# P times V in tiles of 64 rows by 32 columns, and four PSUM banks in place of five for the shared tiles

## The chip, the cores and the metric

The kernel runs on one core of one Trainium2 chip. The metric is the device time of one execution in microseconds, the median of 3 runs. The engines are named as the profile names them: PE (the matrix engine; PEld is its weight load), DVE (vector), ACT (scalar), POOL, SP, and the DMA queues. A matmul multiplies a stationary operand (loaded first) by a moving one that streams through, and adds into PSUM, which has eight banks of 128 partitions by 512 float32.

## The reference

Two branches read the same layer-normed input of 2048 rows by 576 columns, and the output joins them:

```
xn  = layernorm(x)                                   # [2048, 576]
q,k,v = split(xn @ wqkv)                             # 32 heads of 18 columns
p   = softmax(q @ k^T * 18**-0.5)                    # 2048 x 2048 per head
s   = (p @ v, heads side by side) @ wo
g   = silu( (relu(xn @ W_gate) * (xn @ W_up)) @ W_down )   # hidden width 4608
out = x + s * g
```

All is float32. The product that the change touches is `p @ v`, one for every head.

## The kernel before, in words

**Stages.** First the projections q, k and v are made and spilled to DRAM. Then comes one long main stage in which two things are interleaved by hand: the gated layer (lines 300 to 410) and the attention (lines 440 to 620). Last come the output projection and the join.

**Units.** The gated layer is cut into 144 units: a group of 512 rows by 128 of the 4608 hidden columns. One unit (`up`, then `up_end`) is 27 pairs of matmuls over 64 rows each into two banks of their own (`pg0`, `pg1`, the pool `psG`); then ACT takes the relu (`r`, L376), DVE the product (`h`, L378), and ACT and POOL split it (`hh`). After every second unit `down` multiplies two units' `hh` by W_down (`py`, eight tiles of six matmuls), which DVE adds to `y` (L407).

**Attention.** It goes by pairs of heads (16 pairs, `u`), by 512 queries (`qc`, four) and by 128 keys (`kt`, sixteen). One head of a pair lies in the partitions 0 to 63, the other in 64 to 127. `max_steps` makes scores into a tile `pm`, and DVE takes their maxima (`mx`, L531). `exp_steps` makes the scores again with the maximum taken off into a tile `psx`, and ACT writes the exponentials as a tile `p` (L582), keys on partitions, both heads side by side. `attend` takes two key tiles at once: four matmuls, one for each key tile and head, whose stationary operand is 32 columns of `va` (18 columns of v and a column of ones, which gives the softmax's sum) and whose moving operand is `p`. Each of the four adds into its own quarter of the partitions of one bank, `po`; so eight calls of `attend` add up all keys of 512 queries.

**finish.** When the last keys are in, ACT copies `po` to `ot` (L538). Later, as a task, PE transposes `ot` (a tile `tp2`), DVE adds the two key tiles' sums (`os`, L545), takes reciprocals and scales (`rc`, `ob`).

**What sets the order.** PE's order is written out by `emit_unit`: for each of the two halves of 64 rows it spreads the unit's 27 matmuls, the `pm` and the `psx` evenly, and issues one step of the lower rows and one of the upper rows in turn. After them come all `attend` calls that are ready, in one block (two to four calls), and in every second unit `down` and the waiting tasks. Nine units make up one pair of heads; so in 135 units there is one block each, and in the last stage 32 more, of one call each. DVE, ACT and POOL take their instructions in the order in which the scheduler places them, strictly one after the other.

**Banks.** The tiles `pm`, `psx`, `py`, `tp`, `tp2` and the projections' own (`pq`, `pv`) share one pool, `psS`, whose banks are handed out in turn; a matmul that begins a tile waits until the reader of the bank's last tile is done.

```
    psS = ctx.enter_context(tc.tile_pool(name="psS", bufs=5, space=PSUM))
    psO = ctx.enter_context(tc.tile_pool(name="psO", bufs=1, space=PSUM))
    psG = ctx.enter_context(tc.tile_pool(name="psG", bufs=2, space=PSUM))
```

Of the kernel before, what the change touches and what calls it, by code (L numbers as in the profile page):

```python
# [9 lines left out]
F32 = mybir.dt.float32  # L10
F32R = mybir.dt.float32r
AF = mybir.ActivationFunctionType
ALU = mybir.AluOpType
AX = mybir.AxisListType
PSUM = bass.MemoryType.PSUM
# [4 lines left out]
def kernel(  # L20
# [10 lines left out]
    nc = tc.nc  # L31
    P = 128
    R = P // 2
    _, S, D = x.shape
# [5 lines left out]
    NT = S // P  # L40
# [6 lines left out]
    VA = 20  # L47
# [15 lines left out]
    def mm(*args, **kw):  # L63
        return tc.keep_in_program_order(nc.tensor.matmul(*args, **kw))  # L64

    def tp(*args):
        return tc.keep_in_program_order(nc.tensor.transpose(*args))  # L67

    consts = ctx.enter_context(tc.tile_pool(name="consts", bufs=1))
    dram = ctx.enter_context(tc.tile_pool(name="dram", bufs=1, space=DRAM))  # L70
    psS = ctx.enter_context(tc.tile_pool(name="psS", bufs=5, space=PSUM))
    psO = ctx.enter_context(tc.tile_pool(name="psO", bufs=1, space=PSUM))
    psG = ctx.enter_context(tc.tile_pool(name="psG", bufs=2, space=PSUM))
    ident = consts.tile([P, P], F32, name="ident")
    make_identity(nc, ident)
# [10 lines left out]
    def shared(name):  # L86
        return psS.tile([P, 512], F32, tag="one", name=name)
# [365 lines left out]
    for i in range(2):  # L453
        va = at.tile([P, NT, VA + 32], F32, name=f"va{i}")
# [80 lines left out]

    def finish(po, dst, then, *args):
        ot = two.tile([P, 512], F32, name="ot")
        nc.scalar.activation(ot, po, AF.Copy)  # L538

        def rest_():  # L540
            ps = shared("tp2")
            for j in range(4):
                tp(ps[:, j * P : (j + 1) * P], ot[:, j * P : (j + 1) * P], ident)
            os = two.tile([P, 8, VA], F32, name="os")
            nc.vector.tensor_reduce(  # L545
                os[:, :, : DH + 1],
                ps.rearrange("p (a i d) -> p a d i", i=2, d=32)[:, :, : DH + 1, :],
                axis=AX.X, op=ALU.add,
            )
            rc = two.tile([P, 8], F32, name="rc")  # L550
            nc.vector.reciprocal(rc, os[:, :, DH])
            for d in dst:
                nc.vector.tensor_tensor(
                    d.rearrange("p t (h d) -> p t h d", d=DH),
                    os[:, :, :DH].rearrange("p (t h) d -> p t h d", h=2),
                    rc.rearrange("p (t h) -> p t h", h=2).unsqueeze(3).to_broadcast([P, 4, 2, DH]),
                    ALU.mult,
                )
            then(*args)

        tasks.append((rest_, ()))
# [27 lines left out]
    po = [None]  # L589

    def attend():

        va, qc, kt, pq, done = ready.pop(0)
        if kt == 1:
            po[0] = psO.tile([P, 512], F32, name="po")
        for i in (0, 1):
            for h in (0, 1):
                s_ = 32 * (2 * h + i)
                mm(
                    po[0][s_ : s_ + 32, :], va[:, kt - 1 + i, h * VA : h * VA + 32], pq[i][:, h, :],  # L600
                    start=(kt == 1), stop=(kt == NT - 1), skip_group_check=True,
                )
        if kt == NT - 1:
            done(qc, po[0])

    def to_dram(u):
        ob = two.tile([P, NT, HW], F32, name="ob", bufs=1)

        def store(qc):
            if qc == NQ - 1:  # L610
                nc.sync.dma_start(od[:, u * HW : (u + 1) * HW].rearrange("(t p) d -> p t d", p=P), ob)

        return lambda qc, po_: finish(po_, [ob[:, qc * 4 : qc * 4 + 4, :]], store, qc)

    def emit_unit(k, ex, ns, mx, nm):
        up_weights(k + 1)
        if k % 2 and k < len(units):
            down_weights(k - 1)
            down_weights(k)
        n = KC * len(PRODUCTS) + ns + nm  # L620
        ps, gens = up(k)
        order = []
        for t in range(2):
            at_ = {}
            for cnt, gen, off in ((nm, mx, 0.0), (ns, ex, 0.25)):
                for i in range(cnt):
                    at_.setdefault(round((i + off + t * 0.5) * (n - 1) / cnt), []).append(gen[t])
            todo, ops = [], []
            for i in range(n):
                todo += at_.get(i, [])  # L630
                ops.append(todo.pop(0) if todo else gens[t])
            order.append(ops)
        for i, (l, r) in enumerate(zip(*order)):
            next(l)
            next(r)
            if i % 12 == 8:
                gate_step()
        up_end(k, ps)
        while ready:
            attend()  # L640
        if k % 2 == 0 and k:
            for _ in down(k - 1):
                pass
            run_tasks()
# [51 lines left out]
    def done15(qc, po_):  # L696
        finish(
            po_, [o5[:, qc * 4 : qc * 4 + 4, d * DT + U15 : d * DT + DT] for d in range(2)], closed.append, qc
        )
# [109 lines left out]
    for n, _ in enumerate(zip(*[exp_steps(NU - 1, h, pp, done15, True) for h in range(2)])):  # L809
        if n % 2:  # L810
            if len(ready) > 1:
                attend()
            run_tasks()
            due = min(due, 1.0) + 2.2
            while due > 0:
                c = next(outs, None)
                if c is None:
                    break
                due -= c
    while ready:  # L820
        attend()
# [31 lines left out]
```

## Time and profile before

| what | value |
|---|---|
| median of 3 runs | 2805.68 us (2805.17 to 2806.87) |
| the profiled execution | 2808.65 us, its span 2806.9 us |
| granted TensorE clock, mean | 0.992 |
| PE, DVE, ACT, POOL busy | 97%, 69%, 52%, 40% of the span |
| chain that ended last | PE 82%, DVE 9%, DMA 3%, issue 3% |
| main stage | about 370 to 2640 us |

Busy is the union of an engine's instructions. PE's instructions overlap each other, so that a busy PE may still be slowed. In a row of groups, `x` is the count, then come the busy time, the mean of one in ns, and the idle time of the engine just before them with what ended it. A row of the timeline gives the start in us, the length, the engine, the line and the tiles; `x8` means eight such in a row.

### The profile page before, as it was taken

The page shows a single profiled execution, that of the slowest core. Times are in us where ns is not written, and L with a number is a line of the kernel's source. Part 1 is how long each engine was busy: PE and PEld are TensorE (multiplying, and loading weights), DVE is VectorE, ACT ScalarE, POOL GpSimd, SP SyncE. Part 2 cuts the span into 40 slices and gives each one's busy share as a digit, 9 for nine tenths or more (in the row PEclk, how much of TensorE's full clock was granted, in tenths as well). Part 3 has the DMA queues.
Part 4 walks back from the last instruction along what each step waited for, and adds up shares of the span by engine and source line. Part 5 has one row for each costly group of instructions (what it writes and reads, how often), then busy time and mean ns, then how long its engine had stood idle before and what let it go on. Part 6 is the DMA issues. An engine that isn't in the chain of part 4 may idle for free.

```text
span 2806.9 us, 55965 instructions
## 1 busy us (share of the span) xinstructions
PE 2729.5 (97%) x22252; PEld 2081.1 (74%) x22252; DVE 1947.0 (69%) x3458; ACT 1470.5 (52%) x2730; POOL 1135.2 (40%) x845
## 2 busy tenths in 40 slices
PE   6998999999999999999999999999999999999988
PEld 4887777777777777777777777777767777777655
DVE  6325977777777777777777777777777777777542
ACT  4321155655565656565555556565645555555554
POOL 2013544444434444444444444444444444444322
PEclk9999999999999999999999999999999999999999
DMA  8745222323262322223252323232432323231344
GB/s 225 186 147 161 69 60 68 76 60 83 58 146 66 83 71 75 61 69 75 65 140 67 83 64 79 63 79 67 102 89 72 78 65 73 66 72 48 82 132 142
DMA packets 309845, 250.22 MB, mean 89 GB/s; under 512 B 76432, under 2 KB 247952, under 8 KB 309584
## 3 DMA queue, kind: packets, MB, share of 16 engines
q1 hardware_dynamic: 297800, 222.16, 32.1%
q10 hardware_dynamic: 10504, 19.76, 2.1%
q0 software_dynamic: 1280, 4.72, 0.4%
q8 instruction: 176, 2.88, 0.4%
q14 instruction: 85, 0.70, 0.1%
HBM read 201.51 MB, written 44.53 MB: 88 GB/s over the span
## 4 chain that ended last, share of the span: by engine, by line
PE 82%; DVE 9%; DMA 3%; issue 3%; ACT 1%; POOL 1%; SPq 1%; ACTq 0%; DVEq 0%; POOLq 0%
PE pg L64 25%; PE py L64 17%; PE po L64 16%; PE pm L64 10%; PE psx L64 8%; DVE mx L531 7%; PE pw L64 2%; PE tp L67 1%; PE pq L64 1%; DMA rgw<-in_A_wqkv_dram 1%; PE pv L64 1%; DVE e L428 1%; DMA x<-xTd 1%; ACT p L582 1%; PE tps L67 0%
## 5 line engine op out<-in xcount | busy, mean ns | idle before, releaser
L64 PE MATMUL pg<-x,gw 64*128 64x512 f32 x7776 | 1446.0, 397 | 14.5 <-DVE h L378 6.1
L531 DVE TENSOR_REDUCE mx<-pm 128x1 f32<-128x512 f32 x2048 | 1312.1, 684 | 175.5 <-PE pm L64 122.2
L582 ACT ACTIVATE p<-psx 128x512 f32<-128x512 f32 x2048 | 1154.0, 599 | 420.6 <-PE psx L64 314.4
L64 PEld LDWEIGHTS pg<-x,gw 64*128 64x128 f32 x7776 | 1079.3, 187 | 107.1 <-DVE h L378 7.7
L64 PE MATMUL pm<-kT,qT 54*128 54x512 f32 x2048 | 841.7, 411 | 3.3 <-DMA qT<-qd 0.9
L64 PE MATMUL psx<-qT,kT 56*128 56x512 f32 x2048 | 767.8, 401 | 4.5 <-DVE mx L531 3.2
L64 PEld LDWEIGHTS py<-dw,hh 128*128 128x128 f32 x3456 | 460.5, 188 | 61.4 <-issue 52.6
L64 PE MATMUL py<-dw,hh 128*128 128x288 f32 x3456 | 478.2, 297 | 0.0
L64 PE MATMUL po<-p,va 128*32 128x512 f32 x4096 | 474.1, 596 | 0.0
L64 PEld LDWEIGHTS pm<-kT,qT 54*128 54x128 f32 x2048 | 380.1, 186 | 124.8 <-issue 70.6
L407 DVE TENSOR_TENSOR y<-py,y 128x288 f32<-128x288 f32 x544 | 247.7, 457 | 316.5 <-PE py L64 316.5
L94 POOL CAST gw<-rg 128x1152 fp32r<-128x1152 f32 x144 | 164.7, 1144 | 652.8 <-PE pg L64 634.4
L64 PEld LDWEIGHTS psx<-qT,kT 56*128 56x128 f32 x2048 | 366.0, 186 | 50.3 <-DVE mx L531 19.0
L95 POOL TENSOR_TENSOR gw<-rg,gw 128x1152 fp32r<-128x1152 f32 x144 | 382.4, 2656 | 11.5
L94 POOL CAST dw<-rd 128x576 fp32r<-128x576 f32 x144 | 95.6, 664 | 636.4 <-PE py L64 277.3
L64 PEld LDWEIGHTS po<-p,va 128*32 128x32 f32 x4096 | 117.1, 109 | 266.5 <-issue 254.4
L500 ACT ACTIVATE nt<-tp 16x128 fp32r<-16x128 f32 x64 | 17.1, 267 | 433.3 <-PE tp L67 421.4
L95 POOL TENSOR_TENSOR dw<-rd,dw 128x576 fp32r<-128x576 f32 x144 | 205.6, 1428 | 11.5
L381 POOL TENSOR_TENSOR hh<-h,hh 128x512 fp32r<-128x512 f32 x144 | 186.5, 1295 | 15.7 <-ACT hh L380 15.7
L378 DVE TENSOR_TENSOR h<-pg,r 128x512 f32<-128x512 f32 x144 | 99.6, 691 | 98.9 <-ACT r L376 87.9
L380 ACT ACTIVATE hh<-h 128x512 fp32r<-128x512 f32 x144 | 90.8, 630 | 119.3 <-DVE h L378 119.3
L376 ACT ACTIVATE r<-pg 128x512 f32<-128x512 f32 x144 | 85.3, 592 | 80.0 <-PE pg L64 62.4
(77 smaller groups left out, 1232.7 us busy)
## 6 DMA issues: line engine op xcount, KB each, us to landing
rg<-in_B_W_gate_dram SPq DMA_DIRECT2D x144, 288.0 KB
rg<-in_B_W_up_dram SPq DMA_DIRECT2D x144, 288.0 KB
rd<-in_B_W_down_dram SPq DMA_DIRECT2D x144, 288.0 KB
x<-xTd SPq DMA_DIRECT2D x54, 256.0 KB
kT<-kd SPq DMA_DIRECT2D x372, 36.0 KB
qT<-qd SPq DMA_DIRECT2D x372, 36.0 KB
qd<-hh ACTq DMA_DIRECT2D x16, 512.0 KB
kd<-hh ACTq DMA_DIRECT2D x16, 512.0 KB
```

The costliest lines, as they stand in the source:

```text
L64: return tc.keep_in_program_order(nc.tensor.matmul(*args, **kw))
L67: return tc.keep_in_program_order(nc.tensor.transpose(*args))
L94: nc.gpsimd.tensor_copy(hi, raw)
L95: nc.gpsimd.tensor_tensor(lo, raw, hi.bitcast(F32), ALU.subtract)
L376: nc.scalar.activation(r, ps[0], AF.Relu)
L378: nc.vector.tensor_tensor(h, ps[1], r, ALU.mult)
L380: nc.scalar.activation(hh[:, 0], h, AF.Copy)
L381: nc.gpsimd.tensor_tensor(hh[:, 1], h, hh[:, 0].bitcast(F32), ALU.subtract)
L407: nc.vector.tensor_tensor(ys[j][:, cs], ps, ys[j][:, cs], ALU.add)
L428: tc.keep_in_program_order(nc.vector.reciprocal(e[:, cs], e[:, cs]))
L531: nc.vector.tensor_reduce(mx[:, h, j, c : c + 1], ps, axis=AX.X, op=ALU.max)
L582: nc.scalar.activation(pts[kt][:, h, :], ps, AF.Exp, scale=SCALE)
```

## The change

The diff, whole:

```
-    psS = ctx.enter_context(tc.tile_pool(name="psS", bufs=5, space=PSUM))
-    psO = ctx.enter_context(tc.tile_pool(name="psO", bufs=1, space=PSUM))
+    psS = ctx.enter_context(tc.tile_pool(name="psS", bufs=4, space=PSUM))
+    psO = ctx.enter_context(tc.tile_pool(name="psO", bufs=2, space=PSUM))
...
     def finish(po, dst, then, *args):
         ot = two.tile([P, 512], F32, name="ot")
-        nc.scalar.activation(ot, po, AF.Copy)
+        nc.scalar.activation(ot, po[0], AF.Copy)
+        nc.vector.tensor_tensor(ot, po[1], ot, ALU.add)
...
         if kt == 1:
-            po[0] = psO.tile([P, 512], F32, name="po")
+            po[0] = [psO.tile([P, 512], F32, name="po") for _ in range(2)]
         for i in (0, 1):
             for h in (0, 1):
                 s_ = 32 * (2 * h + i)
-                mm(
-                    po[0][s_ : s_ + 32, :], va[:, kt - 1 + i, h * VA : h * VA + 32], pq[i][:, h, :],
-                    start=(kt == 1), stop=(kt == NT - 1), skip_group_check=True,
-                )
+                for t in range(2):
+                    rr = slice(t * R, t * R + R)
+                    mm(
+                        po[0][t][s_ : s_ + 32, :], va[rr, kt - 1 + i, h * VA : h * VA + 32], pq[i][rr, h, :],
+                        start=(kt == 1), stop=(kt == NT - 1), skip_group_check=True,
+                    )
```

Each of the four matmuls of `attend`, over 128 keys, becomes two over 64 keys, one of the lower and one of the upper half of the partitions. They add into the same quarter of the partitions of two different banks. `finish` copies the one bank with ACT as before and adds the other with DVE. The bank for this comes from the shared pool, which goes from five to four.

Two places of the order show it. On PE, at the end of a unit of the second pair of queries, before (the names are those of the section above; the numbers are buffers):

```order
L64 MATMUL pg_5211<-x,gw 128x512
L64 MATMUL pg_5212<-x,gw 128x512
L64 MATMUL po<-p,va_2839 32x512 x8
L64 MATMUL pm<-kT_2829,qT 128x512
L64 MATMUL pg_5379<-x,gw 128x512
```

and in the change:

```order
L64 MATMUL pg_5270<-x,gw 128x512
L64 MATMUL pg_5271<-x,gw 128x512
L64 MATMUL po<-p,va_2839 32x512 x16
L64 MATMUL pm<-kT_2829,qT 128x512
L64 MATMUL pg_5447<-x,gw 128x512
```

The block of P times V has twice as many instructions and stands where it stood; nothing else of PE's order moves.

On DVE, where a `finish` falls at the end of a unit that has no `down`, before:

```order
L531 TENSOR_REDUCE mx<-pm 128x1 x3
L378 TENSOR_TENSOR h<-pg_5660,r 128x512
L531 TENSOR_REDUCE mx<-pm 128x1 x14
L378 TENSOR_TENSOR h<-pg_5853,r 128x512
L407 TENSOR_TENSOR y<-py,y 128x288 x8
```

and in the change:

```order
L531 TENSOR_REDUCE mx<-pm 128x1 x3
L378 TENSOR_TENSOR h<-pg_5745,r 128x512
L531 TENSOR_REDUCE mx<-pm 128x1
L539 TENSOR_TENSOR ot<-po,ot 128x512
L531 TENSOR_REDUCE mx<-pm 128x1 x13
L378 TENSOR_TENSOR h<-pg_5955,r 128x512
L407 TENSOR_TENSOR y<-py,y 128x288 x8
```

The new addition stands behind the next unit's first maximum and ahead of its other thirteen. Where a `down` follows, it stands ahead of the eight additions to `y`.

A third place is the same in both kernels; it is shown because the prediction reads the trace against it. It is PE's order inside a unit, before, with `pg0` and the `psx` and `pm` of one head on one half of the rows and `pg1` and those of the other head on the other half, in turn:

```order
L64 MATMUL psx_10566<-qT_7810,kT3_2827 128x512
L64 MATMUL pg1_10525<-x_10310,gw_10292 128x512
L64 MATMUL pg0_10524<-x_10310,gw_10292 128x512
L64 MATMUL pg1_10525<-x_10324,gw_10292 128x512
L64 MATMUL pg0_10524<-x_10310,gw_10292 128x512
L64 MATMUL pm_10573<-kT8_2837,qT_9927 128x512
L64 MATMUL pg0_10524<-x_10324,gw_10292 128x512
L64 MATMUL psx_10577<-qT_7810,kT3_2827 128x512
```

Nothing moved here: one instruction of the one half of the rows and one of the other half alternate throughout.

## The prediction

> **What bounds the kernel now.** I read the page first, then the busy time by stretches, then PE's timeline around a block of P times V, then the waits.
>
> ```profile
> span 2806.9 us, 55965 instructions
> PE 2729.5 (97%) x22252; PEld 2081.1 (74%) x22252; DVE 1947.0 (69%) x3458; ACT 1470.5 (52%) x2730; POOL 1135.2 (40%) x845
> PE 82%; DVE 9%; DMA 3%; issue 3%; ACT 1%; POOL 1%; SPq 1%; ACTq 0%; DVEq 0%; POOLq 0%
> ...
> 370.00:1300.00 930.00, 927.01 (x7563) 703.22 (x7556) 691.06 (x1205) 530.84 (x972) 406.19 (x295) 1.00 0.31 76
> 1300.00:2640.00 1340.00, 1332.74 (x10827) 1005.90 (x10827) 1000.65 (x1754) 759.89 (x1393) 581.88 (x427) 1.00 0.30 75
> ```
>
> PE is the bound: in the main stage (370 to 2640 us, the last two rows) it is busy all but 10 of 2270 us, at full clock. DVE and ACT are not, on average. But DVE ends 9% of the chain, so PE does wait for it in places. Whatever the change does is therefore read at two points: how long PE streams P times V, and how often PE waits for a bank.
>
> **P times V itself.** The groups, and PE's timeline around two blocks:
>
> ```profile
> L64 PE MATMUL po<-p,va 128*32 128x512 f32 x4096 | 474.1, 596 | 0.0
> ...
> 1515.56 0.63 PE L64 MATMUL pg<-x,gw 64*128 64x512 f32 x2
> 1516.11 0.64 PE L64 MATMUL po<-p,va 128*32 128x512 f32 x4
> ...
> 1518.28 1.47 PE L64 MATMUL po<-p,va 128*32 128x512 f32 x12
> 1519.68 0.50 PE L64 MATMUL pm<-kT,qT 54*128 54x512 f32 x1
> ...
> 1520.02 0.40 PE L64 MATMUL psx<-qT,kT 56*128 56x512 f32 x1
> ...
> 1496.11 1.92 PE L64 MATMUL po<-p,va 128*32 128x512 f32 x16
> 1497.96 0.54 PE L64 MATMUL py<-dw,hh 128*128 128x288 f32 x2
> ```
>
> The program makes 2048 such calls (16 pairs of heads, 4 groups of queries, 8 calls of `attend`, four matmuls) and the trace has 4096 records, so each is two passes. Four records last 0.64 us together where one lasts 0.60: the four column tiles start within 0.02 us and run side by side. Twelve last 1.47 us, so three such groups are (1.47 - 0.61) / 2 = 0.43 us apart. 1024 groups at 0.43 us are 440 us.
>
> The change makes 2048 calls of 128 rows into 4096 of 64 rows. Before, four tiles of 128 by 32 fill the array; after, eight of 64 by 32 fill the same array and stream the same 512 columns. If the eight run side by side, a group is eight records and still 0.43 us: **0 us**. That two halves of the rows run side by side, and don't wait for each other, is shown in other matmuls:
>
> ```profile
> 806.70 0.39 PE L64 MATMUL pg<-x,gw 64*128 64x512 f32 x1
> 806.74 0.39 PE L64 MATMUL psx<-qT,kT 56*128 56x512 f32 x1
> 806.92 0.44 PE L64 MATMUL pg<-x,gw 64*128 64x512 f32 x2
> 807.15 0.40 PE L64 MATMUL pm<-kT,qT 54*128 54x512 f32 x1
> 807.21 0.39 PE L64 MATMUL pg<-x,gw 64*128 64x512 f32 x1
> 807.39 0.39 PE L64 MATMUL psx<-qT,kT 56*128 56x512 f32 x1
> ```
>
> Matmuls of 0.39 us start two in every 0.23 us. And against the order shown above (a `psx`, four `pg`, a `pm`) one `pg` starts 0.04 us ahead of the `psx` that stands before it, and the last `pg` 0.06 us after the `pm` that stands behind it. So the two halves have queues of their own. No row shows rows and columns cut at once. I take 0; the bounds are a gain of 52 us and a loss of 72 us, both worked out next and under the rivals.
>
> **Changing tiles.** A third group begins at 1518.28 + 0.86 = 1519.14, and `pm` could start 0.43 us later, at 1519.57; it starts at 1519.68, and the next of its half 0.34 us on, where 0.23 is usual. So leaving the block costs 0.11 + 0.11 us. Entering costs 0.09: the second `pg` starts at 1515.79 (0.63 less 0.40 us after the first), `po` 0.32 us later in place of 0.23. There is one block in each of 135 units and 32 in the last stage: 167 x 0.31 = 52 us. After the change the rows (64) agree on both sides and only the columns differ. Does that save it? `po` to `py` keeps the rows (128) and changes the columns: sixteen records from 1496.11 are four groups, whose last would be through at 1496.11 + 0.46 + 3 x 0.43 = 1497.86, and `py` starts at 1497.96, 0.10 us late just as `pm` is. So the columns alone cost it, and I take 0 saved. The Trainium skill ("TensorEngine Tiling (Array Packing)", Key Properties) says that changing the tiling mode, and not merely the tile, drains the engine. By that rule too nothing is saved; if only the rows counted, the sum would be 52 us lower. The trace agrees with the rule.
>
> **The shared banks, five to four.** This term decides. The readers, and a place where PE waits today:
>
> ```profile
> L531 DVE TENSOR_REDUCE mx<-pm 128x1 f32<-128x512 f32 x2048 | 1312.1, 684 | 175.5 <-PE pm L64 122.2 <-PE pg L64 26.6
> L582 ACT ACTIVATE p<-psx 128x512 f32<-128x512 f32 x2048 | 1154.0, 599 | 420.6 <-PE psx L64 314.4 <-PE pm L64 17.2 <-PE pg L64 14.6
> ...
> 1507.86 0.74 DVE L428 RECIPROCAL e<-e 128x96 f32<-128x96 f32 x1
> 1508.52 0.63 DVE L531 TENSOR_REDUCE mx<-pm 128x1 f32<-128x512 f32 x1
> ...
> 1508.43 0.40 PE L64 MATMUL psx<-qT,kT 56*128 56x512 f32 x1
> 1508.43 0.63 PE L64 MATMUL pg<-x,gw 64*128 64x512 f32 x2
> 1509.20 0.50 PE L64 MATMUL pm<-kT,qT 54*128 54x512 f32 x1
> ...
> PEld psx L64 <- DVE mx L531: 19.0, 42, 0.9
> PEld pm L64 <- DVE mx L531: 18.7, 52, 0.6
> ```
>
> A reciprocal of the gate puts DVE behind; the maximum of an older `pm` ends at 1509.15, and only then, 0.05 us later, may `pm` at 1509.20 start in its bank. With four banks the `psx` one tile earlier, at 1508.43, needs that bank and waits 0.77 us. So the wait isn't new in kind: it comes one tile sooner.
>
> Three steps give its size. First, for each of the 4864 tiles of the pool that follow another in their bank I took the start of its first matmul less the end of the reader of the tile that four banks would put before it. With five banks the shortest distance is the 0.05 us above; with four, 1022 fall below it, by 164 us in all. Second, that counts one late reader several times, since the first wait moves the rest: in each stretch in which the reading engine never idles I keep the longest alone, and join stretches of DVE and ACT that overlap. That leaves 82 us in 300 stretches. Third, 19.0 + 18.7 = 38 us are waited today (the last two rows) and move forward with the rest. 82 - 38 = **44 us**, between 0 (all of it falls where PE waits anyway) and 164 - 38 = 126 us. I take the middle step, because readers that are late together are the rule, as in the example.
>
> **The addition in finish.** 64 times DVE adds a bank to `ot`. The nearest row is the product `h`, one bank and one SBUF operand of the same shape:
>
> ```profile
> L378 DVE TENSOR_TENSOR h<-pg,r 128x512 f32<-128x512 f32 x144 | 99.6, 691 | 98.9 <-ACT r L376 87.9 <-ACT nx L495 9.8 <-POOL dw L95 1.0
> L407 DVE TENSOR_TENSOR y<-py,y 128x288 f32<-128x288 f32 x544 | 247.7, 457 | 316.5 <-PE py L64 316.5
> 470.04 0.60 ACT L538 ACTIVATE ot<-po 128x512 f32<-128x512 f32 x1 [1.38 <-PE po L64]
> 470.36 2.08 DVE L531 TENSOR_REDUCE mx<-pm 128x1 f32<-128x512 f32 x3 [2.36 <-PE pm L64]
> 1505.07 0.49 PE L64 MATMUL pm<-kT,qT 54*128 54x512 f32 x1
> PE tp L67 <- ACT ot L538: 5.8, 5, 1.5
> ```
>
> In 29 of the 64 `down` follows, and DVE waits 317 / 544 = 0.58 us ahead of each of its eight additions: 0.69 us is hidden there. Were the cover gone, it would be 20 us. In 30 the next unit follows: ACT's copy ends at 470.64, DVE's first maximum at about 471.05, then the addition, 0.69 us, and behind it queue thirteen maxima, for whose banks PE waits. How much of 0.69 us reaches PE: a full unit's 14 `pm` and 16 `psx` take 11.04 us (1505.07 to 1516.11), so four tiles pass in 1.47 us, of which matmul, maximum and release take 0.40 + 0.68 + 0.05; 0.34 us are left. 30 x (0.69 - 0.34) = **10 us**, between 0 and 21. In the last stage PE has nothing else to do five times (last row): 5 x 0.74 = **4 us**. ACT's work is the same, and no DMA is added.
>
> **The sum.** The profiled execution took 2808.65 us, 3 us over the median of the runs. 2808.65 + 0 + 44 + 10 + 4 = 2867; less 3, **2864 us**, 2.1% slower.
>
> **Rivals.** *The row halves of a column take turns once.* If the second pass on the lower rows holds back the first on the upper rows that stands behind it, the upper rows run one pass late through the block, and each block is one pass longer: 167 x 0.43 = 72 us, 2936 us. Against it is the early start at 806.70; for it, that this was seen in full columns alone. The Trainium skill ("TensorE: Matmul & The Clock Gate", Part 3, The mechanism) says that matmuls start and end strictly in program order, which would give this or worse; the early start by 0.04 us disagrees. *Only four of eight run at once:* 440 us more, 3304 us; against it stand both halves of the argument, four columns and two rows side by side. *No change of tile any more:* 52 us less, 2812 us; against it `po` to `py`. *A pass over 64 rows streams faster*, the case on the other side: if it takes the 0.23 us of the matmuls over 64 rows, 1024 x 0.20 = 205 us go, 2659 us; it decides once a pass is under 0.43 - 58 / 1024 = 0.37 us. Against it: those matmuls are one record for each call, not two, so it is another kind of pass.
>
> **Chances.** Forecast 0.60 (2835 to 2900 by itself), turns 0.18, four at once 0.07, no change of tile 0.08, faster pass 0.05, something else 0.02. The range leaves out the faster pass, four at once and the rim of the turns: 2812 to 2945 us. A measurement of this kernel tells 0.2% (5.6 us) from no change. Faster is the faster pass and a little of the saved change of tile: 0.07; within 0.2%, the rest of that with both DVE terms near 0: 0.05; slower 0.88.
>
> **What would show it.** Right: `po` with 8192 records in groups of eight, 0.43 us apart, a block of four calls still 3.57 us to the next `pm`; PE's waits for `mx` about 80 us in place of 38, and some for `p`. Wrong: blocks of 4.0 us (turns), of 7 us (four at once) or under 3 us; `pm` following `po` without the 0.11 us; or bank waits that stay at 38 us.

## The result, and the profile after

The changed kernel takes **2881.66 us** (median of 4 runs, 2879.57 to 2883.58), the kernel before 2805.43 us beside it: a ratio of **1.0272, 95% interval 1.0254 to 1.0290**, so 76 us slower. The forecast was 2864 us, 58 us slower, in a range of 2812 to 2945 us.

The page of the changed kernel, and the main stage in its busy time by stretches:

```profile
span 2881.6 us, 63976 instructions
PE 2802.6 (97%) x26348; PEld 2079.1 (72%) x26348; DVE 1996.9 (69%) x3522; ACT 1500.7 (52%) x2730; POOL 1138.1 (39%) x845
PE 85%; DVE 10%; DMA 2%; ACT 1%; issue 1%; SPq 1%; POOL 0%; DVEq 0%; POOLq 0%; ACTq 0%
...
370.00:1300.00 930.00, 925.64 (x8878) 681.04 (x8876) 691.16 (x1199) 524.48 (x940) 396.99 (x288) 1.00 0.29 74
```

The kind of bound is the same: PE busy 97%, granted clock 1.00 in the stretch, DVE 10% of the chain where it was 9%. In the same 930 us PE gets through less beside P times V, so the stage gets longer. Where it does is read from the first and last starts of three tiles, before:

```profile
L64 PE MATMUL po<-p,va x4096: 592/592/710, 367.9 to 2785.6; 128*32 128x512 f32 x196
L64 PE MATMUL pm<-kT,qT x2048: 386/396/628, 241.7 to 2633.6; 54*128 54x512 f32 x187
L64 PE MATMUL pw<-wo,o5T x64: 288/295/610, 2701.0 to 2801.0; 128*128 128x288 f32 x64
```

and after (in such a row stand the count, the shortest, median and longest in ns, and the first and last start):

```profile
L64 PE MATMUL po<-p,va x8192: 589/589/786, 371.1 to 2858.9; 64*32 64x512 f32 x200
L64 PE MATMUL pm<-kT,qT x2048: 386/397/628, 241.0 to 2700.9; 54*128 54x512 f32 x187
L64 PE MATMUL pw<-wo,o5T x64: 288/294/609, 2769.6 to 2875.0; 128*128 128x288 f32 x64
```

From the first `po` to the last `pm`, which I call the main stage below, it is 2265.7 us before and 2329.8 after: **+64**. From the last `pm` to the last matmul it is 167.4 and 174.1: **+7**. The first `po` came 3 us later, which isn't shown to be the change's: in the experiments whose shared pool has four or five banks, it lies anywhere from 363 to 371 us.

**P times V** is a small part of this. PE's timeline in a window 0.36 us long, and then around whole blocks:

```profile
1531.25 0.66 PE L64 MATMUL po<-p,va 64*32 64x512 f32 x8
...
1531.25 1.09 PE L64 MATMUL po<-p,va 64*32 64x512 f32 x16
...
1531.25 1.95 PE L64 MATMUL po<-p,va 64*32 64x512 f32 x32
1533.13 6.63 PE L64 MATMUL py<-dw,hh 128*128 128x288 f32 x48
...
1566.71 3.66 PE L64 MATMUL po<-p,va 64*32 64x512 f32 x64
1570.31 6.64 PE L64 MATMUL py<-dw,hh 128*128 128x288 f32 x48
```

Eight records last 0.66 us together, sixteen 1.09, thirty-two 1.95: a group of eight every 0.43 us, as the groups of four before. So eight tiles of 64 by 32 run side by side. A block of two calls takes 1.88 us to the next matmul (1533.13 - 1531.25), where it was 1.85 (1497.96 - 1496.11), and a block of four calls 3.60 in place of 3.57. Over all 90 blocks of four calls the medians are 3.594 and 3.571 us: 0.023 us more, in 167 blocks 4 us.

**The waits for a bank**, in the view of the waits (us in total, times, longest):

```profile
PEld pm L64 <- DVE mx L531: 77.8, 242, 2.0
PEld psx L64 <- DVE mx L531: 26.5, 98, 0.7
PEld psx L64 <- ACT p L583: 15.0, 70, 0.5
...
PE tp L67 <- DVE ot L539: 9.1, 5, 2.1
```

Waits for `mx` go from 37.7 to 104.3 us and from 94 to 340 times. Waits of `psx` for `p` that were hardly there (0.3 us) come to 15.0, while the 7.3 us for which `pm` waited for `p` before are gone. The last row is the addition in the last stage, where PE waited 5.8 us for ACT's copy before. The groups show the same from another side:

```profile
L64 PE MATMUL pm<-kT,qT 54*128 54x512 f32 x2048 | 866.5, 427 | 9.6 <-DVE mx L531 5.2 <-DMA qT<-qd 0.7
L64 PE MATMUL psx<-qT,kT 56*128 56x512 f32 x2048 | 821.6, 420 | 2.6 <-DVE mx L531 1.4
```

before:

```profile
L64 PE MATMUL pm<-kT,qT 54*128 54x512 f32 x2048 | 841.7, 411 | 3.3 <-DMA qT<-qd 0.9 <-DVE mx L531 0.6
L64 PE MATMUL psx<-qT,kT 56*128 56x512 f32 x2048 | 767.8, 401 | 4.5 <-DVE mx L531 3.2
```

The same `pm` and `psx` last 16 and 19 ns longer on average. In the timeline of the changed kernel this is the difference between a matmul of 0.39 or 0.40 us and one of 0.50 us. PE and DVE in one stretch:

```profile
1524.54 0.40 PE L64 MATMUL pm<-kT,qT 54*128 54x512 f32 x1
...
1524.77 0.40 PE L64 MATMUL psx<-qT,kT 56*128 56x512 f32 x1
1524.83 0.50 PE L64 MATMUL pm<-kT,qT 54*128 54x512 f32 x1
...
1525.43 0.49 PE L64 MATMUL psx<-qT,kT 56*128 56x512 f32 x1
1526.03 0.50 PE L64 MATMUL pm<-kT,qT 54*128 54x512 f32 x1
...
1523.50 3.07 DVE L531 TENSOR_REDUCE mx<-pm 128x1 f32<-128x512 f32 x5
```

DVE's five maxima are (3.07 - 0.68) / 4 = 0.60 us apart and end at 1524.18, 1524.78, 1525.37, 1525.97 and 1526.57. The `pm` at 1524.83, the `psx` at 1525.43 and the `pm` at 1526.03 each start 0.05 to 0.06 us after one of these ends: PE goes at DVE's pace. Exactly these three last 0.49 to 0.50 us; the two ahead of them, which didn't wait, last 0.40.

### The profile page after: what moved, and what is told of

Same layout as the page of the kernel before. It is cut to its first block, busy times and chain, and to the rows that moved or that the text cites. A ratio compares the mean times of both kernels' runs of the same rounds, so it can differ in the third digit from the quotient of the medians.

```text
span 2881.6 us, 63976 instructions
## 1 busy us (share of the span) xinstructions
PE 2802.6 (97%) x26348; PEld 2079.1 (72%) x26348; DVE 1996.9 (69%) x3522; ACT 1500.7 (52%) x2730; POOL 1138.1 (39%) x845
## 4 chain that ended last, share of the span: by engine, by line
PE 85%; DVE 10%; DMA 2%; ACT 1%; issue 1%; SPq 1%; POOL 0%; DVEq 0%; POOLq 0%; ACTq 0%
PE pg L64 25%; PE py L64 16%; PE po L64 16%; PE pm L64 11%; PE psx L64 9%; DVE mx L531 7%; PE pq L64 2%; PE pw L64 2%; PE pv L64 2%; PE tp L67 1%; DVE e L428 1%; DMA rgw<-in_A_wqkv_dram 1%; PE tps L67 1%; ACT p L583 0%; SPq L130 0%
## 5 line engine op out<-in xcount | busy, mean ns | idle before, releaser
L64 PE MATMUL pg<-x,gw 64*128 64x512 f32 x7776 | 1493.5, 399 | 11.0 <-DVE h L378 5.3
L583 ACT ACTIVATE p<-psx 128x512 f32<-128x512 f32 x2048 | 1183.6, 598 | 462.2 <-PE psx L64 343.4
L64 PEld LDWEIGHTS pg<-x,gw 64*128 64x128 f32 x7776 | 1068.2, 187 | 85.2 <-DVE h L378 7.0
L64 PE MATMUL pm<-kT,qT 54*128 54x512 f32 x2048 | 866.5, 427 | 9.6 <-DVE mx L531 5.2
L64 PE MATMUL psx<-qT,kT 56*128 56x512 f32 x2048 | 821.6, 420 | 2.6 <-DVE mx L531 1.4
L64 PE MATMUL po<-p,va 64*32 64x512 f32 x8192 | 478.2, 593 | 0.0
L64 PEld LDWEIGHTS po<-p,va 64*32 64x32 f32 x8192 | 136.6, 106 | 250.7 <-issue 239.8
```

Of the source, the lines that this page charges most:

```text
L583: nc.scalar.activation(pts[kt][:, h, :], ps, AF.Exp, scale=SCALE)
```

## The experiments

The theory: three separate costs, banks first, then the addition, then the tiles. The rival: that the cut into tiles itself costs the time (turns, changes of tile).

**1. Banks alone.** Before, with one bank less and the eighth unused:

```
-    psS = ctx.enter_context(tc.tile_pool(name="psS", bufs=5, space=PSUM))
+    psS = ctx.enter_context(tc.tile_pool(name="psS", bufs=4, space=PSUM))
```

> The kernel before with the shared pool cut to four banks and nothing else (P times V in four tiles of 128 by 32, one bank, no addition). Theory (the fifth bank is what is lost): +50 to +62 us, about 2860 us; the matmuls that wait for a bank go from 157 to about 600, and the waits of PE's weight load for mx from 38 us to about 90. Rival A (the cut into twice as many tiles costs): at most +15 us. Rival B (the addition on DVE costs): at most +15 us.

Measured: 2861.19 us, ratio 1.0190 (1.0173 to 1.0206): **+54 us**, 53 of them in the main stage. Its waits:

```profile
PEld pm L64 <- DVE mx L531: 66.4, 212, 2.1
PEld psx L64 <- DVE mx L531: 22.3, 74, 0.7
PEld psx L64 <- ACT p L582: 18.3, 90, 0.5
```

Without any change to P times V nearly the whole picture of the changed kernel's waits is there. The missing bank is 70% of the loss (54 of 76 us).

**2. Banks and addition.** The same, and in `finish` DVE adds `po` to its own copy (numerator and denominator of the softmax both double, and the quotient stays):

```
         nc.scalar.activation(ot, po, AF.Copy)
+        nc.vector.tensor_tensor(ot, po, ot, ALU.add)
```

> As the run with four banks, and DVE also adds the bank of P times V to its copy in finish, 64 times (it adds the same bank again, so that sums and denominators both double and the quotient stays). Against the change only the cut into tiles of 64 rows is missing. Theory: 4 us under the change (its blocks are 0.02 us longer, 167 of them), that is 2874 to 2880 us, and 8 to 15 us over the run with four banks alone. Rival A: 20 us or more under the change. Rival B: 40 us or more over the run with four banks alone.

Measured: 2874.89 us, 1.0239 (1.0223 to 1.0256): 14 us over experiment 1, and 7 us under the changed kernel. By the traces the addition is 6.1 us in the main stage and 5.1 in the last; what is left to the changed kernel, 4.9 us in the main stage, is put down to the tiles, of which the longer blocks above are 4. These are differences of one profiled execution each, and the four executions of this experiment alone lie between 2871.87 and 2879.60 us, so such a share is good to some us only.

**3. The addition alone**, with five banks (only the second diff).

> The kernel before with its five shared banks and the addition on DVE in finish alone. Theory: the addition puts DVE behind by 0.69 us thirty times, and the fifth bank gives 0.37 us more of slack, so that most of it is hidden: +3 to +8 us, 2808 to 2813 us (about 4 of it from five finishes in the last stage). Rival B: +40 us or more. Rival A says nothing here.

Measured: 2813.96 us, 1.0024 (1.0015 to 1.0034): +6.4 us; in the profiled execution 2.3 in the main stage and 5.4 in the last. By the traces the addition costs the main stage a third of what it costs with four banks; the medians, 6.4 and 14 us, point the same way.

**4. The addition on POOL.** In the changed kernel ACT copies both banks, and POOL adds the copies (each of the two tiles has one buffer, where `ot` had two):

```
-        nc.vector.tensor_tensor(ot, po[1], ot, ALU.add)
+        nc.scalar.activation(ou, po[1], AF.Copy)
+        nc.gpsimd.tensor_tensor(ot, ot, ou, ALU.add)
```

> The change, but the second bank is copied by ACT into a second tile and POOL adds the two tiles (one buffer for each in place of two), so that DVE is free of the addition. Theory: 8 to 12 us under the change, 2870 to 2874 us, if ACT's second copy (0.60 us, 64 times) holds up no exponentials that PE waits for; the bank waits stay. Rival B: at or near the time of before, 2805 to 2820 us. Rival A: no difference from the change.

Measured: 2893.86 us, 1.0306 (1.0288 to 1.0325), 12 us over the changed kernel. The expectation missed. A group and its waits:

```profile
L541 POOL TENSOR_TENSOR ot<-ot,ou 128x512 f32<-128x512 f32 x64 | 82.5, 1290 | 18.1 <-ACT ou L540 18.1
...
PE tp L67 <- POOL ot L541: 20.6, 5, 9.0
...
PEld psx L64 <- ACT p L585: 30.2, 116, 0.6
```

POOL takes 1.29 us for what DVE does in 0.69, and one transpose waited 9 us for it: the last stage grew by 16 us. In that longest wait ACT's second copy ended at 2701.99 us and POOL's addition began at 2708.59; in between POOL was at work on the weights `wo` of the output projection, so there it was POOL's order and not its pace. What the single buffers add, no run separates. The main stage got shorter, by 4.4 us where the addition had cost 6.1; `psx` waits 30.2 us for `p`, 15.0 in the changed kernel, so it seems that the second copy moved some of the lateness to ACT. As far as single executions show it, most of the addition's price in the main stage does go with it, but the last stage takes back more than that.

**5. Three banks**, one execution, to see how the cost of a bank grows (`bufs=3` in the kernel before).

> The kernel before with the shared pool cut to three banks, a larger dose. Theory: the same reckoning from the trace of before that gave 82 us less 38 us for four banks gives 392 less 38 = 354 us for three, so 3160 us, with waits for p (ACT) as large as those for mx (DVE). If banks are not what PE waits for, the time would stay near that of four banks.

Measured: 3230.14 us, +424 us, where the tally of the prediction, made for three banks, gave 354.

```profile
PEld psx L64 <- DVE mx L531: 245.0, 748, 1.8
PEld pm L64 <- ACT p L582: 101.6, 417, 0.4
PEld pm L64 <- DVE mx L531: 98.2, 353, 0.7
PEld psx L64 <- ACT p L582: 89.8, 261, 1.2
```

The tally is too small here as well, and by about the same share: 354 / 424 = 0.83, and 44 / 54 = 0.81 for the first bank. Not all of it lies where the first bank's loss lay: the main stage grew by 357 us, the time ahead of the first `po` by 37 and the last stage by 27.

**6 to 8. The late reader taken away.** The prediction's example was a reciprocal of the gate that puts DVE behind. The gate, 1 / (1 + exp(-y)), can be had as 0.5 + 0.5 tanh(y / 2) from ACT and POOL, with nothing on DVE:

```
-            tc.keep_in_program_order(nc.scalar.activation(e, y, AF.Exp, scale=-1.0))
+            tc.keep_in_program_order(nc.scalar.activation(e, y, AF.Tanh, scale=0.5))
             yield
-            tc.keep_in_program_order(nc.vector.tensor_scalar(e, e, 1.0, None, op0=ALU.add))
+            nc.gpsimd.tensor_scalar(e, e, 0.5, 0.5, op0=ALU.mult, op1=ALU.add)
             for n in range(6):
                 yield
-                cs = slice(n * GP, (n + 1) * GP)
-                tc.keep_in_program_order(nc.vector.reciprocal(e[:, cs], e[:, cs]))
```

This edit in the kernel before, in the one with four banks, and in the changed kernel:

> The kernel before with five banks, where the gate's sigmoid is made as 0.5 + 0.5 tanh(y/2) by ACT and POOL, so that DVE loses 96 reciprocals of 0.735 us and 16 additions of 0.45 us. It is the same function. Theory (PE waits for a bank because something on DVE puts a maximum late): fewer late maxima, so PE's waits for mx fall from 38 us to about 20, and the time by 15 to 30 us, to 2775 to 2790 us. If the waits come from the maxima's own pace instead, less than 5 us.

> Four banks and the tiles of before, with the gate's reciprocals off DVE as above. Theory: with four banks every late maximum costs more, so the same removal is worth more than with five: 30 to 45 us under the run with four banks alone. If the maxima's own pace is what waits, less than 10 us.

> The change, with the gate's reciprocals off DVE as above. Theory: 30 to 45 us under the change, about 2842 us; if the waits come from the maxima's own pace, less than 10 us.

Measured: **2777.16 us**, 0.9895 (0.9881 to 0.9910); 2828.36 us, 1.0080 (1.0065 to 1.0095); 2851.01 us, 1.0159 (1.0142 to 1.0175). The edit is worth 29 us with five banks, 33 with four, 31 in the changed kernel. The first of the three beats both kernels. Its groups and waits:

```profile
L64 PE MATMUL psx<-qT,kT 56*128 56x512 f32 x2048 | 764.3, 398 | 0.0
...
PEld pm L64 <- ACT p L580: 8.9, 23, 0.5
PEld pm L64 <- DVE mx L529: 7.0, 22, 0.4
```

96 reciprocals and 16 additions, 68.9 + 7.2 = 76 us of DVE's work, are gone, and PE's waits for `mx` fall from 38 us to 7.2. So a late DVE is the cause of most of the waits for `mx` in the kernel before. But the gain hardly depends on the number of banks. With four banks (the second of the three) these waits stay:

```profile
PEld pm L64 <- DVE mx L529: 49.7, 192, 0.6
PEld psx L64 <- ACT p L580: 15.9, 82, 0.5
PEld psx L64 <- DVE mx L529: 6.0, 36, 0.5
```

The loss of the fifth bank therefore needs no reciprocal: without them it is 2828.36 - 2777.16 = 51 us, where it was 54. What puts the readers late then, no run separates. The five maxima shown above aren't an example of it: in the changed kernel one of the gate's instructions on DVE ends just ahead of them, at 1523.58 us, and the next starts at 1526.49.

**9 to 11. Banks of their own.** If readers of two engines hold each other's banks in one shared turn, `psx` (read by ACT) could get a pool apart, and the rest another:

```
-    psS = ctx.enter_context(tc.tile_pool(name="psS", bufs=5, space=PSUM))
+    psS = ctx.enter_context(tc.tile_pool(name="psS", bufs=3, space=PSUM))
+    psX = ctx.enter_context(tc.tile_pool(name="psX", bufs=2, space=PSUM))
```

The kernel before with 3 and 2 banks, the changed kernel with 2 and 2, and experiment 6 with 3 and 2:

> The kernel before with its five shared banks divided: psx (read by ACT) takes two in turn, pm, py and the transposes (mostly read by DVE) three; a pair of the projections takes one of each. Theory (a late maximum holds back the tiles of the other reader, because the banks go round in one turn): pm comes every 0.79 us, so three banks give 2.37 us for 0.40 + 0.68 + 0.05, a slack of 1.2 us in place of 0.7, and psx has 1.38 us for 1.05. PE's waits for mx fall from 38 us to under 10, with waits for p of up to 15 us; 2780 to 2795 us. Rival (the common turn isn't the cause, the number of banks is): 2800 us or more, since psx now has only two.

> The change with its four shared banks divided two and two in the same way. Theory: pm has 2 x 0.79 = 1.58 us for 1.13, a slack of 0.45 us in place of 0.34, and a late maximum no longer holds back psx: 10 to 25 us under the change, 2857 to 2872 us, still far over before. Rival: as slow as the change or slower, because two banks for each reader are fewer than four for both.

> Both steps on the kernel before: the gate's reciprocals off DVE, and the five banks divided three and two. Theory: without the reciprocals only about 20 us of bank waits are left, so dividing adds less than alone: 5 to 12 us under the run with the gate off DVE, 2765 to 2772 us. Rival: the division costs, 2780 us or more.

Measured: 2859.15 us, 1.0193 (1.0178 to 1.0209); 3004.15 us, 1.0714 (1.0698 to 1.0730); 2850.04 us, 1.0163 (1.0146 to 1.0180). All three lost, against the expectation, by 55, 122 and 73 us against the same kernel with one pool. The waits of the first:

```profile
PEld psx L64 <- ACT p L583: 82.7, 238, 1.1
PEld pm L64 <- DVE mx L532: 31.1, 80, 1.2
```

With two banks of its own `psx` waits 82.7 us for ACT, which the shared pool had at 0.3 us. It no longer waits for `mx` (19.0 us before), but `pm`, with three banks to itself, waits 31.1 us for it, where it was 18.7. The loss isn't mainly in the main stage: in the profiled execution the main stage is 13 us longer and the last stage 35, where no `pm` uses the other three banks and `psx` still has its two; 42.3 of its 82.7 us are there. With two and two banks the main stage itself grows, by 74 us. So in these divisions a bank that either reader may leave late was worth more than one kept for each. That the shared turn itself is the trouble isn't borne out by them; other divisions weren't run.

## Why the prediction was right or wrong

| step | forecast, us | measured, us | from |
|---|---|---|---|
| tiles of 64 by 32 | 0 | 5, of it 4 the longer blocks | trace, changed kernel less experiment 2 |
| change of tile saved | 0 | 0 | trace |
| banks, five to four | 44 | 54 (53 in the main stage) | experiment 1 |
| addition, main stage | 10 | 6 | trace, experiments 2 and 1 |
| addition, last stage | 4 | 5 | trace, experiments 2 and 1 |
| sum | 58 | 70 by these rows, 76 by the medians | |

The rows of the trace leave out the start of the main stage, which moves by some us from run to run. By medians alone the three steps are 54 for the bank, 14 for the addition (experiment 2 less 1) and 7 for the tiles (the changed kernel less experiment 2); they fall 2 us short of the 76, because the kernel before took 2807.55 us beside these experiments and 2805.43 beside the changed kernel.

**Tiles: right.** The groups of eight come 0.43 us apart, so "row halves take turns", "four at once" and "a faster pass" are all refuted. The small miss is the eight starts: they come some 7 ns apart, so that the eighth starts 0.05 us after the first, where four took 0.02. The Trainium skill ("TensorE: Matmul & The Clock Gate", Part 3, Measured speedup vs the span model) gives about 4 ns a tile; an estimate from it for the four added starts is 0.016 us a block, and 0.023 was measured.

**Changing tiles: right.** From the last start of a block to the next matmul it is 0.519 us (median), before 0.522. The step that only the columns count, taken from `po` to `py`, held, and so did the rule that the Trainium skill gives in "TensorEngine Tiling (Array Packing)", Key Properties: both sides having 64 rows saved nothing.

The Trainium skill's strict program order ("TensorE: Matmul & The Clock Gate", Part 3, The mechanism), weighed as a rival at 2936 us, isn't what the trace shows, if the two passes of a call stand together in the program: with it the upper rows' first pass couldn't start ahead of the lower rows' second, and eight records would not start within 0.05 us. The records don't name their pass, so that condition is not shown.

**Banks: right in place and mechanism, too small by 10 us.** This is the term that missed most. The place was right: waits for `mx`, some for `p`, caused by one bank less alone. The example was not typical of this loss: without the reciprocals the bank still costs 51 us (experiments 7 and 6). The Trainium skill warns of this side of such a cut ("TensorEngine Tiling (Array Packing)", Gotcha 1: PSUM Pressure: row tiles write to banks of their own); experiment 1 puts 54 us on it here. The step that failed is the tally's price of a wait, which was its lateness only. I measured, in the stretches where only `pg`, `pm` and `psx` run, each `pm` or `psx` that starts within 0.06 us of its bank's release: the time since its half's last matmul, and the time to its half's next one, each less the undisturbed 0.231 us.

| | before | four banks | after |
|---|---|---|---|
| such waits | 153 | 564 | 596 |
| median time since the last matmul, us | 0.466 | 0.260 | 0.258 |
| lateness, summed, us | 34 | 64 | 74 |
| median time to the next matmul, us | 0.337 | 0.337 | 0.337 |
| delay of the next, summed, us | 19 | 61 | 64 |

In these stretches the lateness itself grew by 30 us with four banks, less than the 44 of the tally. The delay of the following matmul, which the prediction had seen only at changes of tile ("0.34 us on, where 0.23 is usual"), grew by 42 us. Half of the 564 waits are under 0.03 us, and each still pays 0.1 us behind it. The two sums together, 72 us, exceed the 53 us by which the main stage grew; the two halves of the rows run side by side, and how much of one half's delay falls where the other waits too isn't separated by any run. By this count 44 us came near 54 partly by luck: it put the lateness too high, and left out the delay behind it. That the number of waits, and not only their length, carries the price is read from these traces; no experiment varied the one without the other.

**Addition: near.** The bounds held. Experiment 3 points to what the prediction didn't have: its price in the main stage seems to depend on the banks, 2.3 us with five and 6.1 with four, by one execution each.

**What would show it**: the 8192 records and the 0.43 us came as written; a block of four calls came at 3.60 rather than 3.57 us; waits for `mx` came to 104 us, not 80, and for `p` in `psx` to 15.

## What to carry to other kernels

Before a PSUM bank is spent on something else, take it away alone and time that: here five banks to four cost 1.9%, and five to three 15% (one execution), more than anything that the new use of the bank did. Price a wait of PE for a bank at its lateness and about 0.1 us for the matmul behind it, so that many tiny waits count by their number; here that is an upper estimate, 72 us for a main stage that grew by 53. Where PE waits for a reader now and then, look for work on that reader's engine that could be elsewhere: an engine that is 69% busy on average was still the one that PE waited for, and 76 us less of its work gave 29 us.

## What the runs showed of the hardware

**A matmul that waited for its bank delays the next one.** In the kernel before, with four banks and after, the next matmul of the same row half comes 0.337 us later (0.332 to 0.342 in the middle 80%), in place of 0.234 where nothing waited; it is over 0.30 us in 93 to 100% of the cases behind a wait and in 1.5 to 4% elsewhere. PE's weight loads in the stretch shown:

```profile
1524.54 0.19 PEld L64 LDWEIGHTS psx<-qT,kT 56*128 56x128 f32 x1
1524.83 0.18 PEld L64 LDWEIGHTS pm<-kT,qT 54*128 54x128 f32 x1
```

The load of the `psx` at 1524.77, which didn't wait, started 0.23 us ahead of its matmul. That of the `pm` at 1524.83, which did, starts with the matmul itself. The view of the waits names the load (PEld) as what waits, so here a matmul that waits for its bank has no weights loaded ahead.

**Eight tiles of 64 by 32 stream as fast as four of 128 by 32**: 0.43 us a group of eight passes over 512 columns, and leaving this tiling for one of 64 rows by 128 columns costs as much as leaving 128 by 32 (0.519 and 0.522 us from the last start to the next matmul).

**The gate's tanh cost ACT hardly more**: 0.69 us an instruction in experiment 6, where the exponential took 0.68, and both kernels load ACT's table twice. The gate's reciprocals had taken DVE 0.73 us for 96 columns each.
